# One tile for two sets of constants, a third buffer for two small tiles, the last output tile whole, and a new order table

## The chip, the cores and the metric

The kernel runs on one core of one Trainium2 chip. The metric is device time in microseconds (us) of one execution; the version before took 213.25 us (median of three runs, 212.79 to 215.01). Engines are named as in the profile: PE (matrix multiply), PEld (its weight load), DVE (vector), ACT (scalar/activation), POOL (GpSimd) and SP (which issues most DMAs).

## The reference, cut to what matters

The input `x` is 2048 rows of 576. The output is the sum of three terms: `x` itself, a spectral filter of the normalised `x`, and a mixture of 64 one-vector experts with 32 routing heads.

```python
x = A_x
xn = _layernorm(x, axis=-1)
return x + _A_ref(xn, A_w_r, A_w_i) + _B_ref(xn, B_w_q, B_k1, B_k2, B_u, B_v)

def _A_ref(x, w_r, w_i):                 # x: 1 x 2048 x 576, w: 2048 x 289
    X = rfft2(x) * (w_r + 1j * w_i)
    return irfft2(X, (2048, 576))

def _B_ref(x, w_q, k1, k2, u, v):        # 32 heads, 8 x 8 experts, the best of each 8
    q = einsum("nd,dhc->nhc", x, w_q)
    s1, s2 = q[..., :128] @ k1.T, q[..., 128:] @ k2.T
    e = argmax(s1) * 8 + argmax(s2)      # per row and head
    act = gelu(einsum("nd,nhd->nh", x, u[e]))
    return einsum("nh,nhd->nd", act, v[e])
```

(The second function is shortened: with one choice per head its softmax is 1.)

## The kernel before, in words

The 2048 rows stand as 16 tiles `t` of 128 rows, all in one SBUF tile `XN`. The 2-D Fourier transform is built of matrix products with constant tables.

**Stage 1, forward along the rows' outer index.** For each tile, `ln` (statistics on DVE, for five tiles on ACT) makes the row scale `rr`. `folds(t)` adds and subtracts mirrored halves of the tile: first into a scratch tile `e` (pool tag `t1`, 128 x 578 words), then into `F` (tag `A2`). It also makes, on ACT, `Rs` = the constant table `Rm` (part of the tile `c32`) times the row scale, and `FL`, a small copy of F's middle columns (tag `yl`). `dft128(t)` multiplies `F` and `FL` by `Rs` on PE, 12 instructions in pairs, and ACT and DVE bring the result from PSUM to the tiles `AB` and `ABL`.

**Stage 2, along the columns and the inner index.** For 16 groups `g`: `d_fwd(g)` multiplies AB and ABL by the column tables `dc` and `dl`; `s_fwd` (two groups at a time) by tables `s16` loaded per group; `s_mul(g)` multiplies by the filter weights `Wt` (DVE, then POOL, then ACT), `s_inv(g)` goes back with the other half of `s16` and writes AB and ABL again.

**Stage 3, back along the columns.** `d_inv(t)` multiplies AB and ABL by the column tables `ic` and `il`; ACT, DVE and POOL unfold the result (scratch tags `t1` and `A2`). `fin(t)` adds the last product and the experts' part in one PSUM tile; a DVE instruction scales it and adds x, and two DMAs of 144 KB write the tile. For `t == 15` the work of `fin` is cut into two halves of the columns: 32 products instead of 16, two DVE instructions and four DMAs of 72 KB.

The four tables `dc`, `dl`, `ic`, `il` lie side by side in one SBUF tile, `c16` (128 x 1737 words), and come by one DMA.

**The experts.** `fold_part(b, s)` multiplies the query weights (32 loads `w` of 576 KB, into five buffers) by the keys; `fold_end`, `fold_last` scale the result to the table `MU`; `x_t(r)` scales transposed input (`xf`); `scores(r)`, `route(r)`, `combine(r)` find the best experts of 256 rows each, with much DVE work, into `CAT`, which `fin` reads.

**What sets the order.** The functions above only record operations. A planner then chooses, engine by engine, which ready operation goes next; a table `RANK` with one number per operation gives the priorities. The result is a fixed order on each engine, and each engine runs its own list strictly in turn, waiting where an input is not there. All recorded instructions therefore carry the same line in the profile, L546, so this text goes by tile names. In the profile `t` stands for the scratch tiles (t1 and t2), `A` for the A2 buffers, `c` for both c16 and c32, `s` for s16. Two lines on what the change touches:

```python
e = T([128, 2, L], F32, "eo", 2, "t1")     # folds: 2 buffers of tag t1, which s_mul and d_inv use too
Rs = T([128, 128], F32, "Rs", 2)           # folds: 2 buffers
```

Of the kernel before, what the change touches and what calls it, by code (L numbers as in the profile page):

```python
# [10 lines left out]
F32 = mybir.dt.float32  # L11
F16 = mybir.dt.float16
# [20 lines left out]
def _consts():  # L33
# [93 lines left out]
    c16 = np.concatenate([dl.reshape(128, -1), ic.reshape(128, -1), il.reshape(128, -1)], 1)  # L127
    c16 = np.concatenate([dc.reshape(128, -1), c16.view(np.float32)], 1)
# [1179 lines left out]
```

## Time and profile before

| what | value |
|---|---|
| median of three runs | 213.25 us (212.79 to 215.01) |
| the profiled execution, device time | 213.16 us |
| its span, first to last instruction | 211.4 us |
| PE busy | 189.9 us (90%) |
| DVE busy | 183.6 us (87%) |
| ACT busy | 129.9 us (61%) |
| POOL busy | 110.4 us (52%) |
| bytes moved by DMA | 48.13 MB |

The device time is 1.76 us longer than the span. Times in the trace count from the span's start. A row of the timeline gives start, duration, engine, operation, tiles written and read, how many instructions are merged (x), and in brackets how long the engine had been idle before and what ended that. A merged row's mean is not its duration over its count where instructions overlap, as on PE and DVE; the distance between starts tells the pace.

### The profile page before, as it was taken

The page shows a single profiled execution, that of the slowest core. Times are in us where ns is not written, and L with a number is a line of the kernel's source. Part 1 is how long each engine was busy: PE and PEld are TensorE (multiplying, and loading weights), DVE is VectorE, ACT ScalarE, POOL GpSimd, SP SyncE. Part 2 cuts the span into 40 slices and gives each one's busy share as a digit, 9 for nine tenths or more (in the row PEclk, how much of TensorE's full clock was granted, in tenths as well). Part 3 has the DMA queues.
Part 4 walks back from the last instruction along what each step waited for, and adds up shares of the span by engine and source line. Part 5 has one row for each costly group of instructions (what it writes and reads, how often), then busy time and mean ns, then how long its engine had stood idle before and what let it go on. Part 6 is the DMA issues. An engine that isn't in the chain of part 4 may idle for free.

```text
span 211.4 us, 6192 instructions
## 1 busy us (share of the span) xinstructions
PE 189.9 (90%) x2408; PEld 130.6 (62%) x2408; DVE 183.6 (87%) x430; ACT 129.9 (61%) x305; POOL 110.4 (52%) x153
## 2 busy tenths in 40 slices
PE   0187799999999999999999999999989999999980
PEld 0175467778767566746666645465644787878850
DVE  2999899955986977988899999999999999999880
ACT  2378998899956884954948974693826622422310
POOL 5526363523088431592518535874836338768750
PEclk9999999999999999999999999999999999999998
DMA  6999999999999999997355062010100001484755
GB/s 197 367 419 410 421 414 416 375 374 399 414 424 407 414 392 401 446 400 302 87 175 158 35 198 67 0 40 0 40 0 2 3 3 28 116 198 113 171 132 150
DMA packets 17453, 48.13 MB, mean 228 GB/s; under 512 B 2192, under 2 KB 8848, under 8 KB 16656
## 3 DMA queue, kind: packets, MB, share of 16 engines
q1 hardware_dynamic: 16848, 47.30, 61.3%
q10 hardware_dynamic: 576, 0.44, 0.7%
q8 instruction: 19, 0.31, 0.6%
q14 instruction: 10, 0.08, 0.1%
HBM read 43.01 MB, written 4.72 MB: 226 GB/s over the span
## 4 chain that ended last, share of the span: by engine, by line
PE 61%; DVE 28%; issue 3%; ACT 2%; DMA 2%; POOL 1%; DVEq 0%; POOLq 0%
PE banks L546 61%; DVE t L546 6%; DVE MT L546 4%; DVE st L546 4%; DVE A L546 3%; DVE w L546 2%; DVE AB L546 2%; DMA XN<-in_x_dram 2%; DVE ABL L546 1%; DVE rr L546 1%; DVE mx L546 1%; DVE mm__96 L546 1%; DVE mv L546 1%; DVE mxr L546 1%; DVE al L546 1%
## 5 line engine op out<-in xcount | busy, mean ns | idle before, releaser
L546 PE MATMUL banks<-MU,xT 128*128 128x512 f16 x192 | 45.6, 379 | 0.6 <-DVE w L546 0.6
L546 PE MATMUL banks<-c,AB 128*128 128x145 f16 (+2 forms) x320 | 37.6, 251 | 0.0
L546 PEld LDWEIGHTS <-xT 128*128 128x128 f16 x224 | 21.1, 98 | 24.5 <-issue 1.5
L546 POOL TENSOR_TENSOR y<-t,t 128x289 f32<-128x289 f32 x32 | 23.8, 766 | 18.4 <-DVE t L546 12.8
L546 POOL TENSOR_TENSOR A<-t 128x287 f32<-128x287 f32 (+2 forms) x42 | 26.2, 641 | 8.8 <-DVE t L546 4.7
L546 POOL TENSOR_TENSOR yh<-y,yh 128x578 f16<-128x578 f32 x16 | 21.2, 1328 | 9.5 <-DVE mxr L546 3.0
L546 POOL TENSOR_TENSOR xT<-xf,xT 128x640 f16<-128x640 f32 x10 | 14.3, 1428 | 22.3 <-DVE A L546 8.2
L546 DVE SCALAR_TENSOR_TENSOR t<-banks,wx,Wt 128x578 f32<-128x578 f32 x32 | 24.6, 811 | 1.4 <-PE banks L546 1.4
L546 PE MATMUL banks<-Rs,yl 128*99 128x128 f32 x64 | 11.0, 305 | 13.0 <-ACT Rs L546 11.2
L546 PE MATMUL banks<-w,KP 128*32 128x288 f32 x256 | 20.5, 415 | 0.3 <-DMA w<-in_wq_dram 0.3
L546 ACT ACTIVATE AB<-banks 128x512 f32<-128x512 f32 (+1 forms) x32 | 18.8, 591 | 0.7 <-PE banks L546 0.7
L546 PE MATMUL banks<-c,ABL 99*128 99x289 f16 (+1 forms) x64 | 18.9, 296 | 0.0
L546 PE MATMUL banks<-Rs,A 128*128 128x128 f32 x128 | 18.7, 297 | 0.0
L546 PEld LDWEIGHTS banks<-c,AB 128*128 128x128 f32 x128 | 18.1, 190 | 0.7
L546 PEld LDWEIGHTS banks<-Rs,yl 128*99 128x99 f32 x64 | 8.3, 180 | 16.5 <-ACT Rs L546 11.9
L546 ACT ACTIVATE yh<-banks 128x290 f32<-128x290 f32 (+1 forms) x16 | 7.2, 457 | 18.2 <-PE banks L546 18.2
L546 PEld LDWEIGHTS banks<-Rs,A 128*128 128x128 f32 x128 | 17.1, 209 | 1.9 <-issue 1.4
L546 DVE TENSOR_REDUCE MT<-w 128x128 bf16<-128x896 bf16 (+1 forms) x16 | 18.1, 1142 | 0.1
L546 POOL TENSOR_TENSOR t<-XN 128x289 f32<-128x289 f32 x14 | 11.5, 824 | 11.4 <-DVE rr L546 3.2
L546 PEld LDWEIGHTS <-AB 128*128 128x128 f16 x192 | 17.0, 146 | 0.1
L546 ACT ACTIVATE A<-banks 128x578 f16<-128x578 f32 (+1 forms) x16 | 10.4, 650 | 8.8 <-PE banks L546 8.8
L546 PE MATMUL banks<-A,s 64*64 64x289 f16 (+1 forms) x320 | 15.6, 336 | 0.0
(131 smaller groups left out, 413.1 us busy)
## 6 DMA issues: line engine op xcount, KB each, us to landing
w<-in_wq_dram SPq DMA_DIRECT2D x32, 576.0 KB, 6.4
xf<-in_xT_dram SPq DMA_DIRECT2D x16, 320.0 KB, 5.2
Wt<-in_W_dram SPq DMA_DIRECT2D x8, 578.0 KB, 6.5
out_dram<-XN SPq DMA_DIRECT2D x28, 144.0 KB, 2.5
XN<-in_x_dram SPq DMA_DIRECT2D x3, 1154.0 KB, 10.3
s<-in_s_dram SPq DMA_DIRECT2D x16, 192.0 KB, 3.5
XN<-in_xd_dram SPq DMA_DIRECT2D x2, 1152.0 KB, 8.3
XN<-in_xd_dram SPq DMA_DIRECT2D x1, 2304.0 KB, 14.0
```

The source lines that it names most:

```text
L546: ins = fn(*[x.place() if isinstance(x, _Ps) else x for x in args], **{k: x.place() if isinstance(x, _Ps) else x for k, x in kw.items()}).ins
```

## The change

It does five things.

1. `c16` shrinks from 1737 to 870 words per row. The first load brings `dc` and `dl` only (435 KB instead of 868.5 KB). A new function `load_ic`, recorded after all of stage 2, loads `ic` and `il` (435 KB) into the same place; it has to wait until the last `d_fwd` has read the old tables.
2. The tag `t1` gets a third buffer. `s_mul` and `d_inv` take their `t1` tiles from the same three.
3. `Rs` gets a third buffer.
4. `fin(15)` goes in one piece, like the others: 16 products, one DVE instruction, two DMAs of 144 KB.
5. The table `RANK` is new, so that the order differs on every engine.

```diff
-    c16 = K([128, 578 + 289 + 580 + 290], F32, "c16")
+    c16 = K([128, 870], F32, "c16")
+    cc = c16.bitcast(F16)
     dc = c16[:, :578].rearrange("p (b l) -> p b l", b=2)
-    cc = c16[:, 578:].bitcast(F16)
-    dl = cc[:, :578].rearrange("p (b l) -> p b l", b=2)
-    ic = cc[:, 578:1738].rearrange("p (b q l) -> p b q l", b=2, q=2)
-    il = cc[:, 1738:].rearrange("p (b l) -> p b l", b=2)
+    dl = cc[:, 1156:1734].rearrange("p (b l) -> p b l", b=2)
+    ic = cc[:, :1160].rearrange("p (b q l) -> p b q l", b=2, q=2)
+    il = cc[:, 1160:].rearrange("p (b l) -> p b l", b=2)
...
-        e = T([128, 2, L], F32, "eo", 2, "t1")
+        e = T([128, 2, L], F32, "eo", 3, "t1")
...
-        Rs = T([128, 128], F32, "Rs", 2)
+        Rs = T([128, 128], F32, "Rs", 3)
...
+    @staged
+    def load_ic():
+        Q.dma_start(c16, a["c16"][:, 870:])
...
-        if t == 15:
-            for n, z in enumerate((slice(0, 144), slice(144, 288))):
...
-            return
...
-    Q.dma_start(c16, a["c16"])
+    Q.dma_start(c16, a["c16"][:, :870])
...
     w_end()
+    load_ic()
...
 RANK = (
-    1031, 1229, 1032, 1219, 1241, 1243, 1242, 1033, 1245, 730, 572, 810, 562, 803, 319, 320, 329, 377, 707,
...
+    818, 1224, 1234, 1225, 1239, 1245, 1244, 1240, 1241, 572, 880, 854, 537, 546, 746, 804, 634, 648, 555,
...
```

What the new order looks like, at three places. (In the built program tiles keep their buffer numbers; the tags' names come first, so that `t1_0_98` is the first t1 buffer, `A2_2_102` the third A2 buffer.)

**DVE, at the start of the program.** The rows are the small operations that make the scales `rr` of the first tiles out of their statistics, and what stands among them. Before (the statistics of tiles 0 and 1 stand just ahead; A2_0 is tile 0, A2_1 tile 1):

```order
L546 RECIPROCAL rr_86<-rr_86 128x1
L546 BN_AGGR mv_87<-st_0_97 128x2
L546 TENSOR_SCALAR rr_86<-rr_86 128x1
L546 TENSOR_SCALAR rr_86<-mv_87,rr_86 128x1
L546 TENSOR_TENSOR A2_0_100<-t1_0_98 128x145
L546 RECIPROCAL rr_86<-rr_86 128x1
L546 TENSOR_TENSOR A2_1_101<-t1_1_99 128x2x144
L546 TENSOR_SCALAR rr_86<-rr_86 128x1
L546 TENSOR_TENSOR A2_0_100<-t1_0_98 128x2x144
L546 TENSOR_SCALAR rr_86<-mv_87,rr_86 128x1
L546 TENSOR_TENSOR A2_1_101<-t1_1_99 128x2x145
L546 TENSOR_SCALAR rr_86<-rr_86 128x1 x2
```

Now (the statistics and the other folds of tile 0 stand just ahead; the first pair of BN_STATS here is that of tile 2, the second that of tile 1; the folds in between, into A2_3 and A2_2, are those of tiles 3 and 2):

```order
L547 TENSOR_TENSOR A2_0_101<-t1_0_98 128x2x144
L547 BN_STATS st_0_97<-XN_67 128x6 x2
L547 RECIPROCAL rr_86<-rr_86 128x1
L547 BN_AGGR mv_87<-st_0_97 128x2
L547 TENSOR_SCALAR rr_86<-rr_86 128x1
L547 TENSOR_TENSOR t1_0_98<-XN_67 128x289 x2
L547 TENSOR_TENSOR t1_2_100<-XN_67 128x289
L547 TENSOR_TENSOR A2_3_104<-t1_0_98 128x2x144
L547 TENSOR_TENSOR A2_2_103<-t1_2_100 128x2x144
L547 TENSOR_SCALAR rr_86<-mv_87,rr_86 128x1
L547 BN_STATS st_0_97<-XN_67 128x6 x2
L547 TENSOR_SCALAR rr_86<-rr_86 128x1
```

The last row of each piece is the operation that finishes tile 0's scale. Ahead of it there now stand the statistics of tile 2, five folds of tiles 3 and 2, and the statistics of tile 1; before, no work of tiles 2 and 3 stood ahead of it.

**SP, the queue that issues the loads, at the start.** The pieces of `XN` are named by size: 577 words is one tile (0, then 1), 1154 is tiles 2 and 3, 2308 is four tiles. Before:

```order
L546 DMA XN_67<-in_x_dram 128x577 x2
L546 DMA kT_69<-in_kT_dram 128x16
L546 DMA s16_2_117<-in_s16_dram 128x384
L546 DMA XN_67<-in_x_dram 128x1154
L546 DMA c32_68<-in_c32_dram 128x320
L546 DMA XN_67<-in_x_dram 128x2308 x3
L546 DMA w_1_120<-in_wq_dram 128x1152
L546 DMA mk_70<-in_mk_dram 128x99
```

Now:

```order
L547 DMA XN_67<-in_x_dram 128x577
L547 DMA c32_68<-in_c32_dram 128x320
L547 DMA XN_67<-in_x_dram 128x1154
L547 DMA XN_67<-in_x_dram 128x577
L547 DMA xf_1_127<-in_xT_dram 128x640
L547 DMA xf_0_126<-in_xT_dram 128x640
L547 DMA XN_67<-in_x_dram 128x2308
L547 DMA kT_69<-in_kT_dram 128x16
```

The table c32 has moved up to the second place, tiles 2 and 3 stand ahead of tile 1, and two loads of xf have moved ahead of the first four-tile piece.

**SP, around the second load of c16, and the end of the output.** Before, late in stage 2 (the two loads of s16 are those of groups 14 and 15):

```order
L546 DMA xf_2_126<-in_xT_dram 128x640
L546 DMA xf_0_124<-in_xT_dram 128x640
L546 DMA s16_2_117<-in_s16_dram 128x384
L546 DMA s16_3_118<-in_s16_dram 128x384
L546 DMA out_0_dram<-XN_67 128x1x288 x28
L546 DMA out_0_dram<-XN_67 128x1x144 x2
```

Now:

```order
L547 DMA xf_2_128<-in_xT_dram 128x640
L547 DMA xf_0_126<-in_xT_dram 128x640
L547 DMA c16_72<-in_c16_dram 128x870
L547 DMA s16_2_119<-in_s16_dram 128x384
L547 DMA s16_3_120<-in_s16_dram 128x384
L547 DMA out_0_dram<-XN_67 128x1x288 x29
```

The new load of c16 stands ahead of the last two loads of s16. The 72 KB stores are gone from the end; of ACT's four last stores (two of 144 KB, two of 72 KB) three of 144 KB are left.

On PE the sequence of stages is the same in both. Around group 11, PE had `s_inv(10)`, `s_fwd(12)`, 16 products of `scores(5)`, `combine(0)`, `s_inv(11)`; now it has `s_inv(10)`, `s_fwd(12)`, `s_inv(11)`. At the end it had `fin(12)`, `combine(7)`, `fin(13)` to `fin(15)`; now it has `combine(7)`, `fin(11)` to `fin(15)`.

More of the change, by code (lines that the diff above doesn't have):

```diff
@@ L126, in _consts @@
         il[:99, b] = np.concatenate([hi[128:161], hi[128:161], lo[128:161]])
-    c16 = np.concatenate([dl.reshape(128, -1), ic.reshape(128, -1), il.reshape(128, -1)], 1)
-    c16 = np.concatenate([dc.reshape(128, -1), c16.view(np.float32)], 1)
+    c16 = [dc.reshape(128, -1), dl.reshape(128, -1).view(np.float32), np.zeros((128, 3), np.float32),
+           np.concatenate([ic.reshape(128, -1), il.reshape(128, -1)], 1).view(np.float32)]
+    c16 = np.concatenate(c16, 1)
     return c32, c16, s16, kk, ll
@@ L1158, in fin @@
         x = XD[:, t]
-        if t == 15:
-            for n, z in enumerate((slice(0, 144), slice(144, 288))):
-                p = PS("bc"[n])
-                for k in range(4):
-                    for h in range(2):
-                        hs = slice(64 * h, 64 * h + 64)
-                        for c in range(2):
-                            cs, ds = slice(64 * c, 64 * c + 64), slice(288 * c + z.start, 288 * c + z.stop)
-                            w, m = ((RT[hs], y[hs, ds]) if k == 0 else
-                                    (CAT[hs, t, 64 * (k // 3):64 * (k // 3) + 64], vS[hs, k % 2 ^ 1, ds]))
-                            P.matmul(p[cs, h, z], w, m, start=(k == 0), stop=(k == 3), tile_position=(64 * h, 64 * c))
-                V.scalar_tensor_tensor(x[:, :, z], p[:, :, z], sc[:, 11:12], x[:, :, z], op0=OP.mult, op1=OP.add)
-                for c in range(2):
-                    (A if c else Q).dma_start(os[t, c, :, :, z], x[64 * c:64 * c + 64, :, z])
-            return
         p = PS("bc"[t % 2])
```

124 rows, old and new, of the table RANK are left out of this document.

## The prediction

> **What bounds the kernel now.** The page says first that PE is the fullest engine and that the chain that ended last runs mostly through it.
>
> ```profile
> PE 189.9 (90%) x2408; PEld 130.6 (62%) x2408; DVE 183.6 (87%) x430; ACT 129.9 (61%) x305; POOL 110.4 (52%) x153
> ...
> PE 61%; DVE 28%; issue 3%; ACT 2%; DMA 2%; POOL 1%; DVEq 0%; POOLq 0%
> ```
>
> A share over the whole span hides where PE's missing 21.5 us (211.4 - 189.9) lie, so I asked for the busy time of each engine by stage. Columns: stretch, its length, busy us of PE, PEld, DVE, ACT, POOL with instruction counts, granted clock, DMA share, GB/s.
>
> ```profile
> 0.00:9.50 9.50, 0.00 (x0) 0.00 (x0) 5.58 (x27) 2.92 (x7) 4.96 (x18) 1.00 0.80 265
> 9.50:15.00 5.50, 5.44 (x24) 5.15 (x24) 5.50 (x23) 3.67 (x10) 1.37 (x4) 1.00 1.01 426
> 15.00:21.50 6.50, 3.97 (x33) 2.99 (x33) 6.47 (x25) 5.65 (x17) 4.22 (x7) 1.00 1.01 406
> 21.50:31.30 9.80, 8.57 (x82) 5.63 (x82) 8.55 (x31) 9.46 (x28) 5.15 (x8) 1.00 1.03 420
> 31.30:50.50 19.20, 19.18 (x189) 14.85 (x190) 15.11 (x44) 17.77 (x45) 8.10 (x10) 1.00 1.01 390
> 50.50:105.00 54.50, 53.78 (x751) 36.00 (x748) 44.36 (x98) 39.65 (x80) 25.98 (x27) 1.00 0.94 374
> 105.00:175.00 70.00, 68.95 (x805) 41.98 (x804) 69.01 (x129) 42.69 (x101) 37.85 (x46) 1.00 0.18 55
> 175.00:205.00 30.00, 29.95 (x537) 23.98 (x534) 28.14 (x58) 8.07 (x23) 22.75 (x36) 1.00 0.52 125
> 205.00:211.40 6.40, 0.04 (x4) 0.00 (x0) 0.88 (x3) 0.00 (x0) 0.00 (x0) 0.86 0.60 165
> ```
>
> PE is idle 13.3 us before 31.3 (9.5 + 0.06 + 2.53 + 1.23), 1.8 us in the 173.7 us from there to 205 (0.02 + 0.72 + 1.05 + 0.05), and 6.4 us at the end. From 31.3 on it is the bound; from 105 to 175 DVE (69.01 of 70) is as full. PE's work hardly changes, so the change is worth what it does to three idle sums: front, middle, tail.
>
> **The front.** PE begins when tile 0's scale is through DVE and ACT has made `Rs`. The chain and the timeline before (start, us, what):
>
> ```profile
> 8.30 0.12 DVE rr L546
> 8.42 0.37 DVE A L546
> 8.79 0.25 DVE rr L546 x2
> 9.04 1.09 DVE st L546 x3
> 10.12 0.24 DVE A L546
> 10.37 0.37 DVE t L546
> ...
> 11.11 0.24 DVE mv L546 x2
> ```
> ```profile
> 9.10 0.68 ACT L546 ACTIVATE Rs<-c,rr 128x128 f32<-128x128 f32 x2
> ...
> 9.54 2.03 PE L546 MATMUL banks<-Rs,yl 128*99 128x128 f32 x8 [9.54 <-ACT Rs L546]
> ```
>
> The scale ends at 9.04, PE starts 0.50 later. In the new order DVE does tile 2's statistics before it, and these need the load of tiles 2 and 3. Its landing is read from the issues and times to landing (the last number) of two loads:
>
> ```profile
> 2.11 0.43 SPq L546 DMA_DIRECT2D s<-in_s_dram  x1
> 2.58 0.43 SPq L546 DMA_DIRECT2D XN<-in_x_dram  x1
> ```
> ```profile
> XN<-in_x_dram SPq DMA_DIRECT2D x1, 577.0 KB, 5.7
> s<-in_s_dram SPq DMA_DIRECT2D x1, 192.0 KB, 3.2
> ```
>
> The s16 load landed at 5.3 with 777 KB queued up to its end, the load of tiles 2 and 3 at 8.3 with 1354 KB. Now it ends at 1025 KB (288.5 + 160 + 577): by the straight line between them 6.6. Bounds: 5.3 and 8.3. DVE has run dry by about 6.0 (tile 0's statistics and folds), so it waits there.
>
> From 6.6 DVE does, at the paces above: two statistics 0.73, a reciprocal 0.1, an aggregate 0.12, a small operation 0.2, five folds at 0.37 (1.85), a small one 0.12, two statistics 0.73, a small one 0.2: 4.05 us, so the scale is ready at 10.65 and **PE starts at 11.15, 1.6 us later than before**. That c32 lands earlier gains nothing then.
>
> PE next needs tile 1's scale, now the last of nine small operations. DVE, from 10.65: two statistics 0.73, two aggregates 0.24, one `t` fold 0.37, four `A` folds 1.2, one PSUM clean-up 0.32, two reciprocals 0.15, nine small ones 1.1: 4.1 us, to 14.75; PE can go on at 15.25. It has been idle since 13.7 (12 products at the slow early pace of 0.213 each, from 11.15). Before, its waits here were:
>
> ```profile
> 11.36 3.62 PE L546 MATMUL banks<-Rs,A 128*128 128x128 f32 x16
> ...
> 15.94 0.68 PE L546 MATMUL banks<-Rs,yl 128*99 128x128 f32 x4 [0.96 <-ACT Rs L546]
> ...
> 18.84 0.68 PE L546 MATMUL banks<-Rs,yl 128*99 128x128 f32 x4 [1.33 <-ACT yl L546]
> ...
> 21.49 0.68 PE L546 MATMUL banks<-Rs,yl 128*99 128x128 f32 x4 [0.26 <-ACT Rs L546]
> ```
>
> Tile 4 began at 21.49. Now the scales of tiles 4 to 7 come after six statistics (2.2), four aggregates (0.5), three `t` (1.1), three PSUM clean-ups (1.0), three `A` (1.1) and their own small ones (0.5): 6.4 us behind 14.75, at 21.15; ACT has a `yl`, then Rs, then a `yl` to do (0.35 each): PE at about 22.2. So four tiles are done as before, 0.7 us later, and one `fold_part` short (0.63 from start to start in the timeline): 1.3 us behind. `fold_part` cannot fill the gaps: 882 KB more stand ahead of its first load, 2.1 us at 420 GB/s, and it landed at 18.5 before, so 20.6 now.
>
> Whether this is made up decides the term. From 21.5 to 50.5 PE idled 1.25 us and ACT 1.77 us in all, and ACT too starts 1.6 us late. Bounds: 0 (all made up) and +2.9 (1.3, and ACT's 1.6 paid again as waits of later tiles). I take **+1.5**, the middle, near the 1.3 that the rows give at 22 us.
>
> The third buffers of `t1` and `Rs` are what lets DVE and ACT run tiles 0, 3 and 2 ahead; by themselves they remove waits of POOL and ACT, off PE's path after 31 us. Price nothing; if that cover is gone, they cost nothing either, since a buffer adds no instruction.
>
> **The middle.** Half the constants now come later. At 410 GB/s the 433.5 KB less in the first load are worth 1.06 us of a full queue, but one load of `Wt` (578 KB, 1.4 us) has moved ahead of the last `w`: nothing. `load_ic` waits for the last `d_fwd`; SP holds only the last two s16 loads behind it, which have to wait for `s_inv(10)` and `s_inv(11)` in any case.
>
> ```profile
> 138.79 0.53 PE L546 MATMUL banks<-c,AB 128*128 128x144 f32 x3
> ...
> 140.37 2.18 PE L546 MATMUL banks<-A,s 64*64 64x289 f32 x32
> 142.48 2.76 PE L546 MATMUL banks<-MU,xT 128*128 128x512 f16 x12
> ```
> ```profile
> 169.19 0.29 PE L546 MATMUL banks<-c,ABL 99*128 99x290 f16 x1
> ```
> ```profile
> c<-in_c_dram SPq DMA_DIRECT2D x1, 868.5 KB, 8.0
> ```
>
> Between the last `d_fwd` (139.3) and the first `d_inv` (169.19) lie 30 us; twice the bytes took 8.0 us in a full queue. Hidden; without that cover it would cost up to 8. `s_inv(11)` has lost the `scores` ahead of it: ACT must first clear `s_inv(10)` and copy `yl`, 0.36 + 0.59 + 0.53 = 1.5 us by the ACT rows, and `s_fwd(12)` covers 2.1 (140.37 to 142.48). For the rest of the new order I see no wait that must come or go: **0**, from -1.8 (all of PE's idle goes) to +1.8 (as much again; DVE is too full to hide more).
>
> **The tail.** What ends last is stores, not arithmetic:
>
> ```profile
> 203.14 0.66 PE L546 MATMUL banks<-A,c 64*64 64x288 f32 x8
> ...
> 203.99 0.43 PE L546 MATMUL banks<-A,c 64*64 64x144 f32 x8
> ...
> 204.67 0.37 PE L546 MATMUL banks<-vS,MT 64*64 64x144 f16 x12
> ```
> ```profile
> 203.36 2.52 DVE L546 SCALAR_TENSOR_TENSOR XN<-banks,sc,XN 128x576 f32<-128x576 f32 x4 [0.25 <-PE banks L546]
> ```
> ```profile
> 203.14 5.31 SPq L546 DMA_DIRECT2D out_dram<-XN  x6
> ```
> ```profile
> 204.21 3.69 ACTq L546 DMA_DIRECT2D out_dram<-XN  x4
> ```
>
> DVE ends at 205.88, SP's last issue at 208.45: ten issues on two queues in 5.31 us, 0.53 each, as if in one line. Now the last five tiles follow one another at 0.88 (0.85 and 0.91 before) with ten stores again: issues end 5.3 us after the first tile's DVE end, the fifth tile's DVE end is 3.5 after it, so 1.8 remain behind DVE instead of 2.57: -0.77. The last tile takes PE 0.88 instead of 1.05 (203.99 to 205.04): -0.17; its DVE instruction ends about 0.08 later after PE. **-0.9**. Bounds: -2.1 (only one issue of 0.55 behind DVE) and +0.8 (the last store of 144 KB lands 1.7 slower than the 72 KB one).
>
> The Trainium skill ("Trainium Kernel Development and Optimization", Key Constraints) says that stores issued from several engines at once save the sequencer's issue time. By that rule ACT's issues would run beside SP's and the tail would gain its full 2.1, for a total near 212.6. The row speaks against it: of SP's last eight issues the slowest took 1898 ns, the median 558.
>
> ```profile
> L546 SPq DMA_DIRECT2D out_dram<-XN x8: 528/558/1898, 199.8 to 207.9; - x8
> ```
>
> **Sum.** The profiled execution took 213.16 us, 0.09 under the median: 213.16 + 1.5 + 0 - 0.9 = **213.8**, no change that a measurement can tell (1%, 211.1 to 215.4, is about what one tells). Its own range is 212.4 to 215.3.
>
> **Rivals.**
> 1. *The front is made up.* For it: PE's 1.25 and ACT's 1.77 us of idle until 50.5, and dft128 of tiles 3 and 2 ready early. Against it: ACT is 97% full from 21.5 to 31.3. It gives 213.16 - 0.9 = 212.3, and 210.5 if the middle's idle goes too. Chance 0.25, a little over half of it below 211.1.
> 2. *ACT's queue carries the delay (slower).* Each tile waits at ACT for Rs and `yl` among other tiles' statistics; with the first Rs 1.6 us late and no room, the later tiles wait once more: 213.16 + 2.9 - 0.9 = 215.2, and with the full middle handing it on (+1) 216.2. It decides if the first Rs ends after 11 us and tile 8 starts after 33 (30.23 before). Chance 0.25.
> 3. *The array stays slow for longer.* Its first 24 products took 0.21 us apart, until 15; eight later ones 1.06 us. A first burst of 2.6 us, then a pause of 1.5, could leave tiles 1, 3 and 2 at the slow pace: two tiles more than before at 12 x 0.1 us, +2.4: 216.2. Chance 0.08. The Trainium skill ("TensorE: Matmul & The Clock Gate", Part 1: The HAM clock gate) has a rule for it: full rate comes after a busy window of about 3.4 us, an idle one takes it away. The trace agrees that the start is slow; that a pause prolongs it no row shows.
> 4. *The change does not do what it says*: the second load of constants is late or buffers are not used. Against it: 30 us of cover. Up to +8: 221. Chance 0.02.
>
> The forecast has 0.40. Faster by over 1%: 0.15, from rival 1. Slower by over 1%: 0.17 of rival 2, all of 3 and 4, 0.03 of the forecast: 0.30. Within: 0.55. The range 211.2 to 216.6 leaves out about 0.1 on either side.
>
> **What would show it.** First PE product at 11.1 (10.2 to 12.5), a wait of over 1 us for Rs after tile 0; PE idle before 31 of 14 to 16 us instead of 13.3; less than 0.1 us of waiting for the new load of c16; ten stores in about 5.3 us, the last issue 1.8 after DVE's end. Wrong if PE starts before 10, or if PE's idle between 50 and 205 moves by over 2 us.

## The result, and the profile after

The changed kernel takes 215.10 us (median of 20 runs, 214.31 to 216.25) where the version before takes 213.14 (20 runs): a ratio of 1.009, interval 1.007 to 1.011. The profiled execution took 214.75 us, with a span of 213.0. The head of its page, with the engines and the chain that ended last:

```profile
PE 189.0 (89%) x2388; PEld 130.8 (61%) x2388; DVE 181.8 (85%) x429; ACT 130.5 (61%) x305; POOL 108.3 (51%) x153
...
PE 72%; DVE 13%; ACT 6%; DMA 3%; issue 3%; SPq 0%; ACTq 0%
```

PE is still the fullest engine, with 0.9 us less work and 2.5 us more idle time. Where both lie is told by busy time by stage, cut at the same four events in both kernels: the first product, the first `d_fwd`, the first `d_inv`, the last product. Before (stretch, its length, busy us of PE, PEld, DVE, ACT, POOL, granted clock, DMA share, GB/s):

```profile
0.00:9.54 9.54, 0.00 (x1) 0.01 (x1) 5.62 (x27) 2.96 (x7) 5.00 (x18) 1.00 0.80 267
9.54:50.51 40.97, 37.17 (x326) 28.62 (x327) 35.58 (x120) 36.53 (x98) 18.80 (x29) 1.00 1.01 404
50.51:169.19 118.68, 116.91 (x1492) 73.05 (x1489) 107.56 (x214) 80.42 (x173) 61.37 (x68) 1.00 0.54 204
169.19:205.04 35.85, 35.79 (x597) 28.89 (x595) 33.99 (x70) 9.97 (x29) 25.20 (x39) 1.00 0.44 105
205.04:211.40 6.36, 0.00 (x0) 0.00 (x0) 0.84 (x2) 0.00 (x0) 0.00 (x0) 0.86 0.60 165
```

After, with the second stretch cut into three:

```profile
0.00:12.11 12.11, 0.00 (x1) 0.01 (x1) 6.63 (x27) 2.40 (x5) 5.78 (x17) 1.00 0.84 281
12.11:22.50 10.39, 8.75 (x48) 8.32 (x48) 10.39 (x43) 7.30 (x21) 3.69 (x9) 1.00 1.02 420
22.50:36.43 13.93, 10.83 (x107) 6.97 (x106) 12.47 (x44) 13.74 (x40) 6.74 (x13) 1.00 0.93 325
36.43:56.22 19.79, 19.50 (x191) 14.06 (x192) 15.14 (x49) 18.70 (x47) 5.84 (x8) 1.00 1.02 397
56.22:172.07 115.85, 115.03 (x1474) 72.73 (x1470) 102.01 (x200) 78.23 (x167) 60.96 (x68) 1.00 0.54 200
172.07:207.02 34.95, 34.85 (x577) 28.71 (x575) 34.33 (x68) 10.08 (x29) 25.32 (x39) 1.00 0.43 104
207.02:213.00 5.98, 0.00 (x1) 0.00 (x0) 0.83 (x2) 0.00 (x0) 0.00 (x0) 0.86 0.73 198
```

Length minus PE's busy time is its idle time. Up to the first `d_fwd` it was 9.54 + 3.80 = 13.34 us and is 12.11 + 1.64 + 3.10 + 0.29 = 17.14: **+3.80**. From there to the first `d_inv` 1.77 and 0.82: **-0.95**. To the last product 0.06 and 0.10; the stores behind it 6.36 and 5.98: **-0.38**. PE's work is **-0.91**, and nearly all of that is the stretch of `d_inv` and `fin` (35.85 to 34.95). The sum is +1.60, the difference of the spans. (The first `d_fwd` itself is 5.71 us later: 3.80 of idle time, and 1.91 of busy time, since two more `fold_part` halves and a few small products now stand ahead of it.)

How the front loses, in PE's timeline (start, us, what, and in brackets the idle time before and what ended it):

```profile
12.11 1.17 PE L547 MATMUL banks<-Rs,yl 128*99 128x128 f32 x4 [12.11 <-ACT Rs L547]
...
16.62 1.17 PE L547 MATMUL banks<-Rs,yl 128*99 128x128 f32 x4 [1.64 <-ACT Rs L547]
...
23.28 0.68 PE L547 MATMUL banks<-Rs,yl 128*99 128x128 f32 x4 [0.72 <-ACT yl L547]
...
35.58 0.27 PE L547 MATMUL banks<-c,bx 128*1 128x128 f32 x1 [0.59 <-DVE bx L547]
36.43 0.68 PE L547 MATMUL banks<-Rs,yl 128*99 128x128 f32 x4 [0.58 <-ACT Rs L547]
```

Tile 0 starts at 12.11 instead of 9.54, tile 1 at 16.62, tile 4 at 23.28 instead of 21.49, tile 8 at 36.43 instead of 30.23. The row of tile 8 before:

```profile
30.23 0.60 PE L546 MATMUL banks<-Rs,yl 128*99 128x128 f32 x4
```

DVE's timeline holds the wait that the new order added:

```profile
7.67 0.82 DVE L547 BATCH_NORM_STATS2 st<-XN 128x6 f32<-128x288 f32 x2 [1.68 <-DMA XN<-in_x_dram]
...
11.42 0.20 DVE L547 TENSOR_SCALAR rr<-rr 128x1 f32<-128x1 f32 x1
```

DVE stands 1.68 us for the load of tiles 2 and 3 (the statistics there are tile 3's, strictly; the two tiles come in one load) and makes tile 0's scale at 11.6.

The second load of c16 is issued 28 us ahead of the first `d_inv`, lands 3.2 us later, and nothing on PE waits for it:

```profile
143.59 0.33 SPq L547 DMA_DIRECT2D c<-in_c_dram  x1
```

In the tail DVE, SP and ACT end like this:

```profile
203.66 4.23 DVE L547 SCALAR_TENSOR_TENSOR XN<-banks,sc,XN 128x576 f32<-128x576 f32 x5
204.50 5.42 SPq L547 DMA_DIRECT2D out_dram<-XN  x7
206.28 2.20 ACTq L547 DMA_DIRECT2D out_dram<-XN  x3
```

Ten stores are issued in 5.42 us; the last issue ends at 209.92, 2.03 us behind DVE's end at 207.89 (2.57 before).

### The profile page after: what moved, and what is told of

It is laid out like the page before. It is cut to its first block, busy times and chain, and to the rows that moved or that the text cites. A ratio compares the mean times of both kernels' runs of the same rounds, so it can differ in the third digit from the quotient of the medians.

```text
span 213.0 us, 6146 instructions
## 1 busy us (share of the span) xinstructions
PE 189.0 (89%) x2388; PEld 130.8 (61%) x2388; DVE 181.8 (85%) x429; ACT 130.5 (61%) x305; POOL 108.3 (51%) x153
## 4 chain that ended last, share of the span: by engine, by line
PE 72%; DVE 13%; ACT 6%; DMA 3%; issue 3%; SPq 0%; ACTq 0%
PE banks L547 72%; DVE t L547 4%; DMA XN<-in_x_dram 3%; ACT t L547 2%; DVE AB L547 1%; DVE A L547 1%; ACT AB L547 1%; ACT Rs L547 1%; DVE mm__96 L547 1%; DVE st L547 1%; DVE MT L547 1%; ACT yl L547 1%; DVE xT L547 1%; DVE w L547 1%; DVE ABL L547 1%
## 5 line engine op out<-in xcount | busy, mean ns | idle before, releaser
L547 PE MATMUL banks<-MU,xT 128*128 128x512 f16 x192 | 45.0, 379 | 0.0
L547 POOL TENSOR_TENSOR A<-t 128x287 f32<-128x287 f32 (+2 forms) x42 | 26.6, 652 | 13.8 <-DVE A L547 4.7
L547 POOL TENSOR_TENSOR y<-t,t 128x289 f32<-128x289 f32 x32 | 23.0, 736 | 19.5 <-DVE t L547 15.4
L547 PE MATMUL banks<-Rs,yl 128*99 128x128 f32 x64 | 11.7, 314 | 16.5 <-ACT Rs L547 14.3
L547 PEld LDWEIGHTS banks<-Rs,yl 128*99 128x99 f32 x64 | 8.8, 189 | 20.2 <-ACT Rs L547 15.3
L547 PEld LDWEIGHTS banks<-Rs,A 128*128 128x128 f32 x128 | 16.9, 209 | 1.9 <-issue 1.9
L547 PEld LDWEIGHTS <-AB 128*128 128x128 f16 x192 | 16.9, 146 | 0.1
L547 POOL TENSOR_TENSOR t<-XN 128x289 f32<-128x289 f32 x14 | 10.7, 766 | 11.2 <-DVE rr L547 4.4
L547 ACT ACTIVATE xT<-xf,bx 128x640 f16<-128x640 f32 x16 | 13.1, 821 | 4.7 <-PE banks L547 4.7
```

The costliest lines, as they stand in the source:

```text
L547: ins = fn(*[x.place() if isinstance(x, _Ps) else x for x in args], **{k: x.place() if isinstance(x, _Ps) else x for k, x in kw.items()}).ins
```

## The experiments

Two theories about the +2.0 us stood at the start. **The front**: everything is lost ahead of stage 2, and the rest of the new order is a gain. **The structure**: the split constants or the third buffers cost something. Inside the front there were again several: the late first product, ACT's list, DVE's list.

Most experiments put one kernel's order into the other. `RANK` is then a list of positions, and the planner takes each engine's operations strictly in that order:

```diff
+        todo = {e: sorted((i for i, o in enumerate(ops) if o.eng == e), key=lambda i: -prio[i]) for e in free}
...
-                if pre[i]:
+                if pre[i] or i != todo[e][0]:
                     continue
...
             wait[e].remove(i)
+            todo[e].pop(0)
```

All results in one table: the median, the ratio to before with its interval, and from PE's timeline of the profiled execution its idle time to the first `d_fwd`, the time from there to the first `d_inv` (PE idle in it), the time from there to the last product, and the stores. The table's own names stand for the orders: old, new. The spans are taken unrounded, so the last column can differ by 0.05 from the rows above.

| kernel | median us | ratio to before | idle in front | d_fwd to d_inv (idle) | d_inv to last product | stores |
|---|---|---|---|---|---|---|
| before | 213.14 | 1 | 13.3 | 118.7 (1.8) | 35.85 | 6.3 |
| changed | 215.10 | 1.009 (1.007 to 1.011) | 17.1 | 115.9 (0.8) | 34.95 | 5.9 |
| e1: changed, old order | 213.72 | 1.003 (1.000 to 1.006) | 14.5 | 118.7 (1.7) | 35.87 | 5.9 |
| e8: e1 with two buffers | 212.63 | 0.997 (0.994 to 0.9995) | 13.3 | 118.7 (1.8) | 35.86 | 5.1 |
| e2: old to 50 us, then new | 215.45 | 1.009 (1.006 to 1.012) | 16.4 | 117.5 (0.8) | 34.98 | 6.4 |
| e3: new to 56 us, then old | 219.17 | 1.027 (1.023 to 1.030) | 18.6 | 119.1 (3.2) | 35.87 | 6.3 |
| e5: old to `scores(2)`, then new, two buffers | 215.81 | 1.010 (1.005 to 1.015) | 13.8 | 118.3 (1.5) | 38.82 | 5.7 |
| e6: new to `scores(2)`, then old | 217.94 | 1.021 (1.016 to 1.026) | 17.2 | 118.1 (2.3) | 35.86 | 5.8 |
| e9: e5, third t1 from stage 2 on | 211.50 | 0.993 (0.991 to 0.995) | 13.2 | 118.7 (2.0) | 34.95 | 5.8 |
| e4: tile 0's scale first | 214.56 | 1.006 (1.003 to 1.009) | 16.9 | 115.8 (0.8) | 34.96 | 5.7 |
| e7: tiles 8 to 11 ahead on ACT | 217.07 | 1.018 (1.014 to 1.023) | 20.2 | 115.9 (0.8) | 34.94 | 5.8 |
| e12: less work on ACT | 214.41 | 1.006 (1.004 to 1.008) | 18.3 | 115.9 (0.8) | 34.95 | 5.9 |
| e10: old to 22 us | 216.16 | 1.016 (1.013 to 1.019) | 17.5 | 115.9 (0.8) | 34.94 | 6.4 |
| e11: old to 36 us | 214.22 | 1.005 (1.002 to 1.009) | 17.0 | 115.8 (0.8) | 34.97 | 5.8 |

Idle time in the front can be compared only where PE's early products ran at the same pace (the last section shows that they do not always). In e3 they ran faster than in the changed kernel: PE is busy 37.63 us up to the first `d_fwd` instead of 39.08 and idle 1.45 us longer, and `d_fwd` comes at 56.22 in both.

### Structure or order

**e1, the changed kernel in the order of before.**

> The changed kernel's tiles (constants in two loads, third buffers, last tile whole), but the order of before on every engine (the new load of c16 stands ahead of the last two s16 loads; three folds of tiles 8, 10 and 12 on DVE and one copy on ACT shift by a few places because the third buffers are handed out in another rotation). If the order alone made the loss: 212.9, that is before less the 0.2 us of the whole last tile, and PE starts at 9.5. If the second load or the buffers cost something: 214 or more, with a wait for c16 near 169 us.

213.72: between the two. Nothing waits for c16, but the front idles 1.2 us more than before. Its timeline shows where that begins (POOL, then DVE):

```profile
17.39 0.98 POOL L548 TENSOR_TENSOR t<-XN 128x289 f32<-128x289 f32 x1
17.74 0.65 DVE L548 SCALAR_TENSOR_TENSOR rr<-mv,rr 128x4 f32<-128x4 f32 x1
```

The third `t1` buffer lets POOL start the fold of tile 5 at 17.39 instead of 18.41. A DVE operation on four columns that starts beside it takes 0.65 us and ends as POOL's does; everything on DVE and, soon after, on ACT is then 0.6 us late.

**e8, the same with two buffers of `t1` and `Rs`**, so that the order of before holds exactly:

```diff
-        e = T([128, 2, L], F32, "eo", 3, "t1")
+        e = T([128, 2, L], F32, "eo", 2, "t1")
...
-        Rs = T([128, 128], F32, "Rs", 3)
+        Rs = T([128, 128], F32, "Rs", 2)
```

> Two buffers of t1 and of Rs and the order of before on every engine, exactly; with the second load of c16 and the last tile whole. If the third buffers made the 0.5 us that the run with the old order and third buffers lost (POOL starts two folds 1 to 2 us earlier there, and a DVE operation beside one of them took 0.65 us instead of 0.15): 213.0, and that operation takes 0.15 again. If the split load made it: 213.7.

212.63, and the two rows read

```profile
17.80 0.15 DVE L548 SCALAR_TENSOR_TENSOR rr<-mv,rr 128x4 f32<-128x4 f32 x1
...
18.40 0.85 POOL L548 TENSOR_TENSOR t<-XN 128x289 f32<-128x289 f32 x1 [0.91 <-DVE A L548]
```

So the split load costs nothing, and the third buffers cost this front 1.2 us of idle time, 1.1 us of the median (213.72 less 212.63, whose intervals do not meet); three folds and one copy that e1 had to shift for the other rotation have a part in that which is not told apart. The whole last tile did not shorten PE's last stretch, 35.86 us.

### Front or rest

In the next runs the order changes from the one to the other in the middle of the program; the place is called the seam.

**e2 and e3, with the seam at the first `d_fwd`.**

> The changed kernel, but up to the first d_fwd every engine runs in the order of before; from there on the new order. If the front is the whole loss (3.8 us of PE's idle time) and the gains behind it (0.9 of waits, 0.7 of busy time, 0.6 in the tail) stand by themselves: 215.1 - 3.8 = 211.3. If the 0.9 of waits went only because PE came late: 212.2. If the loss is not in the front: 214 or more.

> The changed kernel, with the new order up to the first d_fwd and the order of before from there on. If the front is the loss: 213.1 + 3.8 - 0.2 = 216.7, or 215.8 if a late PE finds its waits of 0.9 us gone here too. If the loss is not in the front: 213 to 214.

Neither came out as a theory had it: 215.45 and 219.17. Of the 3.1 us that PE idles more in e2's front than before, about 1.2 are those of the third buffers, as in e1. What is left is at the seam. At 50 us the two orders have done different work. In e2 PE waits for small operations that the new order did long before (its timeline at the seam):

```profile
52.50 0.27 PE L548 MATMUL banks<-c,wm 128*2 128x128 f32 x1 [0.82 <-ACT t L548]
55.11 0.18 PE L548 MATMUL banks<-id,mxr 128*128 128x2 f16 x1 [1.23 <-DVE mxr L548]
```

**e5 and e6, with the seam at the first product of `scores(2)`**, where the two orders differ by a dozen small operations. (The expectations put it at about 103 us; in the profiles it stands at 113 to 118.)

> Two buffers of t1 and of Rs as before, and the order of before until the first product of scores(2) (about 103 us, where both orders have done the same work but for a dozen small operations); from there the new order, the second load of c16 and the whole last tile. If the front is the loss and the later gains (0.9 of waits, 0.7 of busy time, 0.5 in the tail) stand by themselves: 213.2 - 2.1 = 211.1. If the 0.9 of waits went only because PE came late: 212.0. If the loss does not lie in the front, as the 215.4 of the run with the earlier seam would say when taken at its word: 215.

> The other half: the changed kernel, new order until the first product of scores(2), the order of before from there. If the front is the loss and the later parts are the gain: 215.1 + 0.7 + 0.5 = 216.3, and 217.2 if the 0.9 of waits for DVE comes back although PE is late. If the loss does not lie in the front: 213.7.

e6, 217.9, is above its range: PE idles 2.25 us between `d_fwd` and `d_inv` although it is late, and stage 3 has its old length of 35.86. e5 brought the front back (13.8; its profiled execution is the slowest of four, with a granted clock of 0.93 in the first 50.5 us). But its stage 3, at a granted clock of 1.00, takes 38.82 us against 34.95 in the changed kernel, and 3.2 of these 3.9 us are three waits in PE's timeline:

```profile
178.82 0.71 PE L548 MATMUL banks<-A,c 64*64 64x288 f32 x8 [1.38 <-DVE t L548]
181.37 0.35 PE L548 MATMUL banks<-c,ABL 99*128 99x290 f16 x1 [0.47 <-DVE t L548]
199.79 0.72 PE L548 MATMUL banks<-A,c 64*64 64x288 f32 x8 [1.35 <-DVE t L548]
```

They name the scratch tile `t`, of which e5 has two buffers of tag `t1` where the new order of stage 3 was made for three.

**e9 gives it back**, from `s_mul` on, and keeps `folds` on two of the three; every engine's list is that of e5:

```diff
+        turn["t1"] = t % 2
         e = T([128, 2, L], F32, "eo", 3, "t1")
```

> Order of before until the first product of scores(2), new order behind it, as in the run with the seam at 103 us, but with three buffers of t1 from s_mul on; folds keeps to two of them, and Rs has two, so that the front runs as before. Theory (the front is the loss; the 3.2 us of waits in stage 3 of that run came from the missing third buffer of t1): scores(2) at 113.4, first d_inv 54.3 to 55.4 later, 35.0 to the last product, 5 to 6 for the stores, together 209.4 to 211.4. If the new order behind 103 us needs the late PE to run well: 213 or more, with waits of 1 us or more before d_inv.

211.50 us: 0.7% faster than before and 1.7% faster than the changed kernel. Its stages:

```profile
9.42:50.41 40.99, 37.17 (x326) 28.61 (x327) 35.66 (x120) 36.53 (x98) 18.81 (x29) 1.00 1.00 395
50.41:169.12 118.71, 116.72 (x1491) 72.94 (x1488) 105.58 (x215) 81.15 (x173) 61.64 (x68) 1.00 0.55 208
169.12:204.08 34.96, 34.85 (x577) 28.71 (x575) 34.34 (x68) 10.06 (x29) 25.33 (x39) 1.00 0.43 103
```

The front is that of before, stage 3 that of the changed kernel. This settles the first question: what stands ahead of `scores(2)`, order and buffers together, costs the changed kernel 3.6 us (215.10 less 211.50; 3.9 of PE's idle time; by the two ratios to before, 1.009 and 0.993, it is 3.4), and the new order of stage 3, with the third `t1` buffer, is worth 0.9 us. Between `scores(2)` and the first `d_inv` PE idles 0.83 us in e9 and 0.06 in the changed kernel: most of the waits that the change took away there are gone only when PE comes late. In the old order a late PE did not help (1.05 before, 1.44 in e6).

### Inside the front

**e4, tile 0's scale ahead of the wait.** On DVE the four small operations of `rr` for tile 0 move ahead of the statistics that wait for tiles 2 and 3.

> The changed kernel with one move on DVE: the four small operations that make tile 0's scale stand behind tile 0's folds, ahead of the statistics that wait for the load of tiles 2 and 3. PE should start near 7 instead of 12.1. If the late start is what costs: 212.5 (2.6 us back). If tiles 1 to 3 and then tiles 8 to 11 are held by DVE's and ACT's own lists: PE waits for tile 1 until about 16 anyway, and the time is 214.7 (at most 0.4 back).

PE's timeline, its first two waits and the start of tile 4:

```profile
7.19 1.17 PE L548 MATMUL banks<-Rs,yl 128*99 128x128 f32 x4 [7.19 <-ACT Rs L548]
...
16.52 1.17 PE L548 MATMUL banks<-Rs,yl 128*99 128x128 f32 x4 [6.45 <-ACT Rs L548]
...
24.12 0.68 PE L548 MATMUL banks<-Rs,yl 128*99 128x128 f32 x4 [0.60 <-ACT yl L548]
```

PE starts 4.9 us earlier, stands 6.45 us instead of 1.64, and goes on with tile 1 at the same time (16.52 against 16.62). From there this profile is not typical: it is that of the slowest of e4's eight executions (215.55), in which PE kept its slow early pace into tile 3, reached tile 4 at 24.12 instead of 23.28 and the first `d_fwd` at 57.06 instead of 56.22. What the move is worth is read from the median, 0.5 us less. **The late first product is at most a small part of what costs.**

**e7, ACT's list.** A few operations of tiles 8 to 11 moved ahead on ACT, DVE and POOL.

> The changed kernel with a few operations of tiles 8 to 11 moved ahead: on ACT the statistics of tile 9 and the square root ahead of those of tile 15, and the sum over Wt (1.17 us) behind the three tables Rs; on DVE the four operations of the scale ahead; on POOL one small one. Tile 0 is left as it is. If ACT's list sets PE from 22 to 36 us: PE's first products of tile 8 come about 2 us earlier and the time is 213.4 to 214.0. If the late start, or DVE's, sets the front: 215.0.

It went the other way: 217.07. 1.7 us of statistics were put ahead of the clean-up of tiles 6 and 5 on ACT. DVE, which has the next step of that clean-up in its own fixed list, stood for it:

```profile
30.01 0.42 DVE L548 TENSOR_TENSOR ABL<-banks,ABL 33x256 f16<-33x256 f32 x1 [1.87 <-ACT ABL L548]
```

From there all of DVE's folds were 2 to 3 us late. Neither theory had the two lists tied together like this.

**e12, less work on ACT with every list as it is**: the ten statistics operations sum over 64 of 576 columns.

```diff
-                A.activation(j, XN[:, t + i, :D], AF.Copy, scale=-1.0 / 13824, accum_out=b)
-                A.activation(j, XN[:, t + i, :D], AF.Square, scale=1.0 / 24, bias=b, accum_out=mv[:, t + i, 1:2])
+                A.activation(j[:, :64], XN[:, t + i, :64], AF.Copy, scale=-9.0 / 13824, accum_out=b)
+                A.activation(j[:, :64], XN[:, t + i, :64], AF.Square, scale=1.0 / 8, bias=b, accum_out=mv[:, t + i, 1:2])
```

> The changed kernel with every list as it is, but less work for ACT: the ten statistics operations on ACT (tiles 7, 9, 11, 13, 15; 0.67 to 0.77 us each in the profile of the changed kernel, between 15.5 and 34 us) sum over 64 of the 576 columns, so that the row scales of these five tiles are estimates. About 0.45 us less for each. If ACT's list holds PE between 22 and 36 us, as the chain of the changed kernel reads (13.7 of 14.7 us on ACT): the seven of them that stand ahead of tile 8's table give up to 3 us, PE's first product of tile 8 comes at 33.5 to 34.5 instead of 36.4, the idle time to the first d_fwd falls by 1.5 to 3 us, 212.2 to 213.7. If DVE's list or the loads hold it: 214.6 to 215.1.

The two groups of operations fell by 4.3 us together, from 7.2 to 2.9 (busy us and mean ns of one; first in this kernel, then in the changed one):

```profile
L548 ACT ACTIVATE t<-XN,rr 128x64 bf16<-128x64 f32 x5 | 1.7, 337 | 0.0
L548 ACT ACTIVATE t<-XN 128x64 bf16<-128x64 f32 x5 | 1.2, 245 | 0.0
```
```profile
L547 ACT ACTIVATE t<-XN,rr 128x576 bf16<-128x576 f32 x5 | 3.8, 765 | 0.0
L547 ACT ACTIVATE t<-XN 128x576 bf16<-128x576 f32 x5 | 3.4, 672 | 0.0
```

PE's first product of tile 8 came at 36.15, not at 33.5 to 34.5. It no longer waits for `Rs`, but a small product that stands ahead of it in PE's list waits for DVE:

```profile
35.77 0.27 PE L548 MATMUL banks<-c,bx 128*1 128x128 f32 x1 [0.93 <-DVE bx L548]
36.15 0.68 PE L548 MATMUL banks<-Rs,yl 128*99 128x128 f32 x4
```

The first `d_fwd` came 0.3 us earlier (55.94), although the load of tiles 2 and 3 landed 0.3 later in this execution, and the median is 0.7 lower. So ACT's amount of work explains about a fifth of the 3.8 us. The chain of waits of the changed kernel had suggested more: of the 14.7 us from 21.7 to 36.4 it runs 9.7 on ACT (not 13.7, as the expectation has it) and 4.5 on PE.

**e10 and e11, the old order to 22 and to 36 us.**

> The changed kernel with the order of before until the first product of tile 4 (22 us), the new order behind it. PE's idle time by 22 us is then 12.1 to 12.8 instead of 13.8. If the first 22 us are the cause, since ACT got 3.3 us less work done in them and has no room afterwards: the waits of 3.4 us between 22 and 56 us shrink to 1.3 as well, 212.0 to 212.8. If the lists between 22 and 36 us make those waits by themselves: they stay, 213.9 to 214.4.

> The same with the seam at the first product of tile 10 (36 to 38 us). PE's idle time to the first d_fwd: 13.3 as before, and 1.1 more for the third buffers in the front (seen with the old order), 14.4 instead of 17.1: 212.4. If the loss came behind 36 us: 215.

216.16 and 214.22, the first outside both of its ranges, the second between its two figures. Both have waits at their seams (2.45 us at 27.2 in e10, 1.91 at 41.9 in e11) and the third buffers in the old front, which cost e1 1.2 us, so they do not tell whether the first 22 us would spoil the rest. What they do say with e2, e3 and e7: a piece of one order does not fit into the other, since each engine's list counts on how far the others are.

**What stays open.** What is common to the changed kernel and every run with its front that loses is DVE's start: in the first 9.5 us it does 4.1 us of work instead of 5.6 (3.8 to 4.5 in those runs), since it waits for tiles 2 and 3, and from 7.7 to 22.5 it never stops. e4 and e12 left that wait in place and gained 0.5 and 0.7 us, and in e12 it is DVE that PE then waits for ahead of tile 8. That this wait is the cause was argued from these rows, not tried by itself; how the 3.8 us split between it and the lists behind it is open.

## Why the prediction was right, and where it was not

The time, 215.1, lies in the range (211.2 to 216.6), in the forecast's own range too (212.4 to 215.3), and the ratio of 1.009 is within the 1% that were called no change, though twenty executions do tell it from none (1.007 to 1.011). The sum, 213.8, was 0.95 us short of the profiled execution's 214.75, and its terms were further off than the sum: +2.3 in the front, -0.95 in the middle, -0.9 in stage 3, +0.5 in the tail. That these errors cancel by two thirds is luck.

- **The front, +1.5, measured +3.8.** The mechanism was right: DVE waits for the load of tiles 2 and 3 ahead of tile 0's scale. The first product came at 12.11 (11.15 forecast, within 10.2 to 12.5). Of the 0.96 us between them the load's landing is the part that failed: 6.6 by the straight line between two loads, 7.67 measured, which was inside the bounds. The line took the loads as served one after the other. DVE's chain behind it was 3.95 us (4.05 forecast), and the wait for tile 1 was 1.64, over 1 us as said. PE's idle time before 31.3 us was 15.1 (14 to 16 forecast). The step that failed is the next one, "bounds: 0 and +2.9; I take +1.5, the middle". Nothing was made up, and from 31.3 to 50.5 us PE lost another 2.1 us where it had lost 0.02 before; +2.9 was no upper bound, since it allowed each late tile one more wait and no more.
- **The third buffers, "Price nothing".** The reason given, "a buffer adds no instruction", does not hold: in the order of before they cost 1.2 us of PE's idle time (e1 against e8), and that loss begins where POOL starts a fold earlier beside DVE's work. How much of the front's 3.8 us is theirs in the new order was not tried.
- **The middle, 0, measured -0.95 of idle time.** In its bounds of -1.8 to +1.8. The second load of c16 is hidden as said. That a late PE would find its waits for DVE gone was not seen; e9 shows that most of this gain hangs on the lateness.
- **The tail, -0.9, measured -0.38, and stage 3, not foreseen ("PE's work hardly changes"), -0.9.** "The last tile takes PE 0.88 instead of 1.05" was wrong: it set a distance between starts against a distance from a start to the end. Whole or in halves the last stretch is the same (e8). The last issue is 2.03 us behind DVE's end, against 1.8 forecast and 2.57 before. The gain in PE's work comes from the order: stage 3 takes 34.95 or so in every kernel with the new order and three buffers, and 35.85 or so in every one with the old. PE changes between `d_inv` and `fin` fewer times; the changed kernel has six groups of `fin`, before had nine. One change in its timeline:

```profile
178.09 0.55 PE L547 MATMUL banks<-c,AB 128*128 128x145 f16 x6
178.47 0.29 PE L547 MATMUL banks<-c,ABL 99*128 99x290 f16 x1
178.60 0.56 PE L547 MATMUL banks<-c,AB 128*128 128x145 f16 x6
179.26 0.72 PE L547 MATMUL banks<-A,c 64*64 64x288 f32 x8
```

  From the start of six `c,AB` products to the next product of `d_inv` 0.38 us pass, to the first of `fin` 0.66. Three groups less at some 0.3 us are the 0.9; that this is the whole of it was not tried.
- **"As if in one line"**, the reading of the stores' issues, was wrong. In e8 the last two, on SP and ACT, run at the same time:

```profile
206.03 0.59 SPq L548 DMA_DIRECT2D out_dram<-XN  x1
206.04 0.58 ACTq L548 DMA_DIRECT2D out_dram<-XN  x1
```

  What had looked like a line in the kernel before were single issues of 1.2 and 1.9 us; there, too, an issue of SP from 205.07 to 206.97 runs beside two of ACT from 205.06 to 206.98. By these rows the rule that the prediction set aside (the Trainium skill, "Trainium Kernel Development and Optimization", Key Constraints: issuing from several engines saves issue time) holds here too. The gain was 0.38 and not the 2.1 that went with that rule: seven of the ten issues stand on SP and took 5.42 us one after another. The stores behind the last product took 5.1 to 6.4 us in kernels whose last issues are the same, so a tail gain of half a microsecond can't be read from one profile.
- **Rivals.** The front was not made up (rival 1). Rival 2 gave 215.2 and both its marks came true, the first `Rs` after 11 us and tile 8 after 33; but its mechanism, ACT's queue, is worth about a fifth by e12. Rival 3, a slow array, did occur in one way (see the last section): in the changed kernel's profile it cost nothing, in e4's 0.84 us at tile 4. Rival 4 fell with the row of c16.

## What to carry to other kernels

In a program where every engine runs a fixed list, the order that is good for one part can be bad for another: compare kernels by stages with cuts at the same events, and when two orders are joined, join them where both have done the same work. An engine that starts late is not necessarily the one that costs; the next place to look is the feeder that has no slack behind its wait. A buffer more is not free: it lets another engine start earlier, beside work that it then slows (up to 1.1 us here), while the order of a later stage may need it (3.9 us of stage 3 here), so hand it out by stage.

## What the runs showed of the hardware that was not expected

**A POOL operation can hold up a DVE operation.** The 4-column operation of e1 took 0.65 us beside a POOL fold and 0.15 without it. The Trainium skill ("SBUF — State Buffer", SBUF: two separate sides) says that a DVE operation with two inputs in SBUF and a POOL operation that reads SBUF shut each other out for a whole instruction; the two rows of e1, which end within 0.02 us of each other, agree. So does the length of the POOL fold, which began beside a DVE fold (17.37 to 17.82): 0.98 us, where the shortest of its kind in e1 took 0.69.

**The slow pace of the array is not a matter of the program alone.** The changed kernel and e3 have the same lists up to 56 us and the same pause of 1.64 us, but tile 1's eight products with `A` took 1.92 us in one and 1.06 in the other, at a granted clock of 1.00 in both (PE's timeline of the changed kernel, then of e3):

```profile
17.59 1.92 PE L547 MATMUL banks<-Rs,A 128*128 128x128 f32 x8
```
```profile
17.14 1.06 PE L548 MATMUL banks<-Rs,A 128*128 128x128 f32 x8
...
23.28 0.68 PE L548 MATMUL banks<-Rs,yl 128*99 128x128 f32 x4 [1.32 <-ACT yl L548]
```

Tile 4 starts at 23.28 in both: the fast one waits 1.32 us there, the slow one 0.72 (the row of the changed kernel is shown above). The Trainium skill ("TensorE: Matmul & The Clock Gate", Part 1: The HAM clock gate) has the busy window run freely, so that it depends on chance where the first product falls in it; that fits these rows.
